# Attention and a token/channel mixer on one core: a hand-set issue order on four engines, strided heads in even steps, the tail product on doubled columns, byte-wise weight conversion

## The chip, the cores and the metric

The kernel runs on one core of one Trainium2 chip, as one program. The metric is device time in microseconds from start to end of the program, the median of several runs. The engines are named as the profile names them: PE multiplies matrices (PEld loads its weights), DVE, ACT and POOL work element-wise, SP issues all DMAs of this kernel. Each engine executes its own list of instructions in a fixed order, and semaphores hold an instruction until what it reads is there.

## The reference

```python
# q, k, v: batch 8, heads 8, sequence 576, head size 64, float32
scores = q @ k.T / sqrt(64)
rel = pos[:, None] - pos[None, :]
mask_local   = (rel >= 0) & (rel < 32)                         # heads 0 to 3
mask_strided = (rel >= 0) & (pos[None] % 32 == pos[:, None] % 32)   # heads 4 to 7
attn = softmax(where(mask, scores, -1e9));  x = heads_side_by_side(attn @ v)   # (8, 576, 512)

xt = x.transpose(0, 2, 1)
h  = relu(xt @ w_tok1) @ w_tok2             # 576 -> 256 -> 576, along the sequence
u  = x + h.transpose(0, 2, 1)
out = u + relu(u @ w_ch1) @ w_ch2           # 512 -> 1536 -> 512, along the channels
```

## The kernel before

**Products in three terms.** Every big product is computed as high*high + high*low + low*high of float32 values split in two, so each weight matrix lies in SBUF as a high and a low tile (w1h and w1l, w2h and w2l, t1, t2). The weights come as raw 64-bit values. `convert` makes float32 words of a piece of 128x512: on ACT one Abs with a scale (L87), on DVE three bit operations (L88, L89, L90). `load_split` then rounds to the high tile on ACT (L101) and subtracts on POOL for the low one (L102). There are 24 such pieces for w1 and w2, and six smaller ones for the token weights.

**Passes.** The channel mixer `mlp` runs nine passes. Passes 0 to 7 take positions 0 to 511 of one batch each, and pass 8 takes the last 64 positions (the tail) of all eight batches. A pass has 24 blocks of 12 matmuls with 512 columns: 12 blocks `up_proj` (L450) and 12 blocks `down_proj` (L462), in the order up 0, up 1, up 2, down 0, up 3, down 1 and so on. After an up block ACT makes gh (L453) and DVE makes gl (L454), which the down block of the same number reads four blocks later. Two PSUM buffers (ps_h) hold the up products.

**Work between the blocks.** During a pass other work is inserted for later passes:

- `tok1` (28 matmuls of 512 columns for a batch, L322) and `tok2` (L345, L337) make the u of the next batch. Before each tok1 step ACT and DVE split a slice of x (L310, L313, L317). `tok2` handles 128 channels at a time: four transposes and six matmuls of 512 columns.
- `tok2_tail` makes the tail of u: for each of four channel groups one transpose (L359) and six matmuls with only 64 columns (L337), kept in the tile utail.
- `local_unit` is local attention for 384 positions of two heads: 24 score matmuls on each of two halves (L133), mask and maximum on DVE (L142), exp on ACT (L145), z on DVE (L148, L149), three transposes (L153), a copy (L155), 48 matmuls (L161), a scaling on DVE (L172). Eighteen units of three chunks fall into the passes.
- Strided attention of batches 0 and 1 runs on PE (`strided_pe`), that of batches 2 to 7 on POOL and DVE (`strided`): for each i from 0 to 17 POOL multiplies i+1 rows (L275), DVE sums them (L276); then a softmax; then 18 products and sums again (L290, L291). A k tile shares its buffer with the output tile of the batch before (sb).

Local and strided results go to HBM and come back as the tile x (`load_x`), of which there is one buffer.

**What sets the order.** Up to the first pass and in the passes, a scheduler orders the instructions of each engine from the calls in the source, their priorities and its own model of time. `at(fc, f)` only says after which up block the source calls an insertion. The strided batches are recorded with a priority lowered by 3000. Local units, tok1, tok2 and the tail share two PSUM buffers (ps_t). Pieces of the weights are called two for each of the first nine fc of pass 0, and the PE-strided lanes of batch 1 in the same pass.

## Time and profile before

| what | value |
|---|---|
| median of 3 runs | 926.01 us (925.93 to 929.34) |
| the profiled execution, whole | 926.17 us |
| its span, first to last instruction | 924.4 us |
| PE busy, share of the span | 850.3 us, 92% |
| DVE, ACT, POOL busy | 479.4, 240.3, 398.9 us |
| mean granted clock of PE | 0.943 |

Matmuls overlap in the pipeline, so "busy" of PE says only when it had something in flight. How fast it goes is read from the distance between the starts of matmuls, and where it stands from the idle time before an instruction, which the views give in brackets with the instruction that ended it. A clock of 1.00 is 2.4 GHz, and 0.5 is 1.2 GHz.

### The profile page before, as it was taken

To read this page: it belongs to the slowest core of one execution; us is meant where nothing else is said; L and a number is where in the kernel's file an instruction comes from. 1 tells how busy PE (TensorE), PEld (TensorE's weight loads), DVE (VectorE), ACT (ScalarE), POOL (GpSimd) and SP (SyncE) were. 2 spreads that over 40 slices of the span, in tenths; PEclk is the share of its full clock that TensorE was granted. 3 is DMA by queue.
4 is the path that set the end of the run, shared out by engine and by line. 5 is a ranking of instruction groups with operands and counts; after the bars stand their busy time and mean duration, and the time that the engine had idled before them with its cause. 6 is when DMAs were issued, how large, how long until landed. Compare 5 with 4: busy or idle time off the path is not lost.

```text
span 924.4 us, 15050 instructions
## 1 busy us (share of the span) xinstructions
PE 850.3 (92%) x5964; PEld 684.7 (74%) x5964; DVE 479.4 (52%) x1133; ACT 240.3 (26%) x700; POOL 398.9 (43%) x291
## 2 busy tenths in 40 slices
PE   5897899569998599999998899999999999999997
PEld 4675688448776487877786678878887888888885
DVE  3969782277648747765775565766223112213111
ACT  5656452122222222222221221232122111111110
POOL 0324540098746848768795765967002000100000
PEclk9568999769999799999999799999999999999999
DMA  8665641411332351133315313042103000001002
GB/s 249 185 220 158 212 128 45 137 46 44 98 116 87 107 146 50 52 114 100 99 27 162 105 45 103 30 133 80 46 1 111 1 1 23 23 1 44 3 0 46
DMA packets 65635, 78.03 MB, mean 84 GB/s; under 512 B 23076, under 2 KB 50340, under 8 KB 65564
## 3 DMA queue, kind: packets, MB, share of 16 engines
q1 hardware_dynamic: 65564, 77.07, 27.7%
q8 instruction: 47, 0.77, 0.4%
q14 instruction: 24, 0.20, 0.1%
HBM read 58.63 MB, written 18.28 MB: 83 GB/s over the span
## 4 chain that ended last, share of the span: by engine, by line
PE 61%; POOL 13%; DVE 10%; DMA 8%; SPq 3%; issue 2%; ACT 2%; POOLq 0%; ACTq 0%; DVEq 0%
PE h L450 25%; PE acc L462 24%; POOL sprod L275 7%; POOL sprod L290 6%; PE t L337 5%; DMA sb<-in_ks 3%; PE t L322 2%; DMA x<-xs 2%; PE t L345 2%; DVE xlo L313 1%; DVE ss L276 1%; DVE w_f L89 1%; DVE w_f L88 1%; DVE lz L148 1%; DMA w_raw<-in_wt 1%
## 5 line engine op out<-in xcount | busy, mean ns | idle before, releaser
L275 POOL TENSOR_TENSOR sprod<-sb,sa 128x64 f32<-128x64 f32 (+8 forms) x108 | 159.5, 1513 | 103.4 <-DMA sb<-in_ks 52.7
L454 DVE SCALAR_TENSOR_TENSOR gl<-h,gh 128x512 fp32r<-128x512 f32 x108 | 74.1, 688 | 208.8 <-ACT gh L453 208.4
L290 POOL TENSOR_TENSOR sprod<-sa,ss 128x64 f32<-128x64 f32 (+8 forms) x108 | 155.0, 1476 | 38.8 <-DVE ss L285 33.5
L462 PE MATMUL acc<-gl,w2h 128*128 128x512 f32 x432 | 171.0, 396 | 0.0
L450 PE MATMUL h<-ul,w1h 128*128 128x512 f32 x432 | 170.4, 395 | 0.5 <-DVE ul L350 0.4
L450 PE MATMUL h<-uh,w1h 128*128 128x512 f32 x432 | 167.1, 396 | 3.8 <-DVE gl L454 3.8
L450 PE MATMUL h<-uh,w1l 128*128 128x512 f32 x432 | 170.1, 394 | 0.0
L462 PE MATMUL acc<-gh,w2l 128*128 128x512 f32 x432 | 169.9, 393 | 0.0
L462 PE MATMUL acc<-gh,w2h 128*128 128x512 f32 x432 | 166.5, 399 | 3.3 <-ACT gh L453 3.3
L453 ACT ACTIVATE gh<-h 128x512 fp32r<-128x512 f32 x108 | 63.8, 596 | 344.9 <-PE h L450 344.9
L473 POOL TENSOR_TENSOR ot<-uh,ul 128x512 f32<-128x512 f32 x32 | 42.8, 1343 | 158.1 <-DMA out_t<-ot 79.8
L276 DVE TENSOR_REDUCE ss<-sprod 128x1 f32<-128x64 f32 (+8 forms) x108 | 84.3, 782 | 49.1 <-POOL sprod L275 48.5
L291 DVE TENSOR_REDUCE sb<-sprod 128x64 f32<-128x64 f32 (+8 forms) x108 | 84.2, 782 | 34.5 <-POOL sprod L290 33.3
L450 PEld LDWEIGHTS h<-uh,w1h 128*128 128x128 f32 x432 | 81.6, 190 | 22.2 <-DVE gl L454 4.7
L462 PEld LDWEIGHTS acc<-gh,w2h 128*128 128x128 f32 x432 | 81.0, 189 | 21.8 <-ACT gh L453 4.3
L450 PEld LDWEIGHTS h<-ul,w1h 128*128 128x128 f32 x432 | 81.9, 190 | 18.6 <-DVE ul L350 1.4
L450 PEld LDWEIGHTS h<-uh,w1l 128*128 128x128 f32 x432 | 81.9, 190 | 17.4
L462 PEld LDWEIGHTS acc<-gl,w2h 128*128 128x128 f32 x432 | 81.1, 188 | 17.4
L462 PEld LDWEIGHTS acc<-gh,w2l 128*128 128x128 f32 x432 | 81.1, 188 | 16.8
L145 ACT ACTIVATE ls<-ls,lm 128x64 f32<-128x64 f32 x144 | 48.3, 337 | 44.6 <-DVE lm L142 44.3
L322 PE MATMUL t<-xh,t1h 128*128 128x512 f32 (+1 forms) x90 | 34.3, 413 | 18.1 <-ACT xh L310 12.8
L337 PE MATMUL t<-t2h,hh 128*128 128x64 f32 (+1 forms) x128 | 49.1, 383 | 0.0
(86 smaller groups left out, 1013.8 us busy)
## 6 DMA issues: line engine op xcount, KB each, us to landing
w_raw<-in_w SPq DMA_DIRECT2D x24, 512.0 KB
out_t<-ot SPq DMA_DIRECT2D x32, 256.0 KB
lv<-in_vw SPq DMA_DIRECT2D x20, 384.0 KB
lk<-in_kT SPq DMA_DIRECT2D x20, 208.0 KB
x<-xs SPq DMA_DIRECT2D x8, 512.0 KB
lq<-in_qT SPq DMA_DIRECT2D x20, 192.0 KB
x<-xl SPq DMA_DIRECT2D x7, 512.0 KB
sa<-in_qs SPq DMA_DIRECT2D x6, 576.0 KB
```

What stands on the lines that cost most here:

```text
L145: nc.scalar.activation(out=s_t[:, c, j, :], in_=s_t[:, c, j, :], func=AF.Exp, bias=m_t[:, c, j:j + 1], scale=-1.0, accum_out=z_t[:, c, j:j ...
L275: nc.gpsimd.tensor_tensor(out=pr, in0=k_t[:, :n, :], in1=q_t[:, i:i + 1, :].to_broadcast([P, n, D]), op=ALU.mult)
L276: nc.vector.tensor_reduce(out=s_t[:, i, :n], in_=pr, axis=AX.X, op=ALU.add)
L290: nc.gpsimd.tensor_tensor(out=pr, in0=v_t[:, :, :n], in1=s_t[:, i:i + 1, :n].to_broadcast([P, D, n]), op=ALU.mult)
L291: nc.vector.tensor_reduce(out=o_t[:, i], in_=pr, axis=AX.X, op=ALU.add)
L322: nc.tensor.matmul(ph[m], l[:, c, ms], r, start=(c == 0 and k == 0), stop=(c == NSC - 1 and k == 1))
L337: nc.tensor.matmul(pu, l[:, cs], r[:, m, ts], start=False, stop=(m == 1 and k == 2), skip_group_check=True)
L450: nc.tensor.matmul(ph, l[:, cc, fs], r, start=(cc == 0 and k == 0), stop=(cc == NCC - 1 and k == 2))
L453: nc.scalar.activation(out=gh, in_=ph, func=AF.Relu)
L454: nc.vector.scalar_tensor_tensor(out=gl, in0=ph, scalar=0.0, in1=gh.bitcast(F32), op0=ALU.max, op1=ALU.subtract)
L462: nc.tensor.matmul(acc[cc], l[:, fc, cs], r, start=(fc == 0 and k == 0), stop=(fc == NFC - 1 and k == 2))
L473: nc.gpsimd.tensor_tensor(out=o_t, in0=uh.bitcast(F32), in1=ul.bitcast(F32), op=ALU.add)
```

## The change

**Order.** From the passes on (the prologue keeps the scheduler) PE, DVE, ACT and POOL issue in the order of the source. SP is still ordered by the scheduler. `mlp` calls `done` after each block, and insertions stand in tables of block numbers 0 to 23: the local units in `UNITS`, tok1 at blocks 14 to 19 (15 to 19 in passes 0 and 1), tok2 at 20 to 23, the tail product after block 0 of the batch's own pass, weight pieces one for each of the blocks 0 to 15 of pass 0, the PE-strided lanes of batch 1 in its blocks 1 to 12.

**Strided heads.** `strided` becomes a generator whose steps multiply two rows that together have 18 (8; 7 and 9; 6 and 10; ...; 17), and whose sums stand one step behind. `some_strided` calls 22/20 of a step's worth for each block in passes 0 and 1, and 22/23 later. q, k, v and the output share three buffers.

**Tail.** `tok2_tail` puts h on the weight side: six matmuls of 512 columns against a t2 with the 64 tail columns doubled, a DVE addition onto x, and a DMA of 64 rows to HBM. In pass 7 all tails are loaded and transposed by 16 transposes (`tail_u`).

**Weights.** `convert` builds the low bits and the sign with byte accesses: a new Identity on ACT (L96), a byte-wise and on DVE (L97), then Abs (L99) and a single combining DVE operation (L100), in place of three.

**Smaller moves.** z and its reciprocal stand after the transposes' copy; tok1 splits two slices ahead; local units have two buffers for k and v.

```diff
-        nc.vector.tensor_scalar(out=a, in0=a, scalar1=3, scalar2=None, op0=ALU.logical_shift_left)
-        nc.vector.scalar_tensor_tensor(out=a, in0=low, scalar=29, in1=a, op0=ALU.logical_shift_right, op1=ALU.bitwise_xor)
-        nc.vector.scalar_tensor_tensor(out=a, in0=high, scalar=0x80000000, in1=a, op0=ALU.bitwise_and, op1=ALU.bitwise_xor)
+        nc.scalar.activation(out=y_b[:, :, 0], in_=raw_b[:, :n, 3], func=AF.Identity, bias=below, scale=1.0 / 32)
+        nc.vector.tensor_scalar(out=y_b[:, :, 3], in0=raw_b[:, :n, 7], scalar1=128, scalar2=None, op0=ALU.bitwise_and)
...
+        nc.vector.scalar_tensor_tensor(out=a, in0=a, scalar=3, in1=y, op0=ALU.logical_shift_left, op1=ALU.bitwise_xor)
...
+    STEPS = ((8,),) + tuple((i, NJ - 2 - i) for i in range(7, -1, -1)) + ((NJ - 1,),)
...
+            late = []
+            for step in STEPS:
+                pr, at = pool.tile([P, NJ * D], F32, name="sprod", bufs=2), 0
+                now = []
+                for i in step:
+                    now.append((i, pr[:, at:at + (i + 1) * D]))
+                    product(*now[-1])
+                    at += (i + 1) * D
+                for l in late:
+                    add(*l)
+                late = now
+                yield at / (NJ * D)
...
+        for m in range(2):
+            hh, hl = h[m]
+            for k, (l, r) in enumerate(((t2h, hh), (t2l, hh), (t2h, hl))):
+                nc.tensor.matmul(pu, l[:, m, MAIN:], r, start=(m == 0 and k == 0), stop=(m == 1 and k == 2))
+        rs = slice(64 * (b % 2), 64 * (b % 2) + 64)
+        nc.vector.tensor_tensor(out=x_t[rs, NSC - 1], in0=pu[rs], in1=x_t[rs, NSC - 1], op=ALU.add)
+        nc.sync.dma_start(out=ud[b], in_=x_t[rs, NSC - 1])
...
+        for p in range(B // 2):
+            nc.tensor.transpose(pu[:, P * p:P * p + P], u_t[:, p, P * cc:P * cc + P], ident)
+        return split_u(pool, pu)
...
+    ordered = {mybir.EngineType.PE, mybir.EngineType.DVE, mybir.EngineType.Activation, mybir.EngineType.Pool}
+    ctx.enter_context(tc.manual_schedule(engines=ordered))
...
+    def some_strided(blocks):
+        turn["owed"] += 22.0 / blocks
...
+    UNITS = {1: ((0, 1, 3, 4), (0, 3, 5, 6), (2, 5, 8, 9), (4, 8, 10, 11)),
+             2: ((0, 2, 5, 6), (0, 4, 8, 9), (4, 7, 11, 12), (6, 10, 12, 13)),
...
+        at(0, tok2_tail, ps_t, x_t, h, b)
+        if b + 1 < B:
+
+            local, stride, steps = (12, 13, (15, 16, 17, 18, 19, 19)) if b < 2 else (11, 11, range(14, 20))
+            at(min(local, stride), load_next, b + 1)
+            at(local, load_half, b + 1, 0)
+            at(stride, load_half, b + 1, 1)
+            for i in steps:
+                at(i, do_tok1)
+            for cc in range(NCC):
+                at(20 + cc, do_tok2, cc)
...
+        if b == 0:
+            for i in range(16):
+                at(i, do_pieces, 1)
```

**ACT in pass 0, where the weight pieces are converted.** L87 or L99 is Abs, L96 the new Identity, L101 or L111 the rounding to the high tile, L453 or L535 makes gh, and L227, L239 are the exps of the PE-strided heads. Before:

```order
L453 ACTIVATE gh<-h 128x512
L87 ACTIVATE w_f<-w_raw 128x512 x2
L227 ACTIVATE es,em<-es,em 126x126 x4
L227 ACTIVATE es,em<-es,em 72x72
L101 CAST w1h<-w_f 128x512
L453 ACTIVATE gh<-h 128x512
L101 CAST w2h<-w_f 128x512
L87 ACTIVATE w_f<-w_raw 128x512 x2
```

After:

```order
L535 ACTIVATE gh<-h 128x512
L96 ACTIVATE w_rest_103<-w_raw,below 128x512
L99 ACTIVATE w_f<-w_raw 128x512
L111 CAST w1h<-w_f 128x512
L239 ACTIVATE es,em<-es,em 126x126 x4
L239 ACTIVATE es,em<-es,em 72x72
L535 ACTIVATE gh<-h 128x512
L96 ACTIVATE w_rest_102<-w_raw,below 128x512
L99 ACTIVATE w_f<-w_raw 128x512
L111 CAST w2h<-w_f 128x512
```

Before, other instructions of ACT stand between Abs and the cast of the same piece; now the cast follows its Abs directly.

**PE at the end of pass 3** (acc is the down product, lv the values of a local unit, x and hh belong to tok2 of the next batch). Before:

```order
L462 MATMUL acc_3422<-gh,w2l 128x512
L161 MATMUL t<-lv,ls 32x64 x24
L345 MATMUL t<-ident,x 128x128 x4
L337 MATMUL t<-t2h,hh_3874 128x512
L337 MATMUL t<-t2l,hh_3874 128x512
```

After, at the end of pass 1 (from pass 1 on every pass ends in this way up to pass 6), with the tail product further on:

```order
L545 MATMUL acc_2143<-gh,w2l 128x512
L404 MATMUL t<-ident,x 128x128 x4
L408 MATMUL t<-t2h,hh_2770 128x512
L408 MATMUL t<-t2l,hh_2770 128x512
L408 MATMUL t<-t2h,hl_2771 128x512
L408 MATMUL t<-t2h,hh_2772 128x512
L408 MATMUL t<-t2l,hh_2772 128x512
L408 MATMUL t<-t2h,hl_2773 128x512
L532 MATMUL h<-uh,w1h 128x512
```

The local unit's last matmuls have moved away from the end of the pass to its blocks 4 to 13.

**POOL, strided products of the first batch that POOL computes** (sprod is the product; ot the sum uh + ul that the output needs). Before:

```order
L275 TENSOR_TENSOR sprod<-sb,sa 128x1088
L473 TENSOR_TENSOR ot<-uh,ul 128x512
L275 TENSOR_TENSOR sprod<-sb,sa 128x1152
L473 TENSOR_TENSOR ot<-uh,ul 128x512 x3
L290 TENSOR_TENSOR sprod<-sa,ss 128x64
L290 TENSOR_TENSOR sprod<-sa,ss 128x128
```

After, the second of these batches:

```order
L312 TENSOR_TENSOR sprod<-sa 128x576
L312 TENSOR_TENSOR sprod<-sa 128x512
L312 TENSOR_TENSOR sprod<-sa 128x640
L549 TENSOR_TENSOR ot<-uh,ul 128x512
L312 TENSOR_TENSOR sprod<-sa 128x448
L312 TENSOR_TENSOR sprod<-sa 128x704
```

Long and short products now alternate, and the sums ot stand singly between them.

## Rows read from the trace of the kernel before

**Rows 1.** The page: the span, and busy time of PE with its share and instructions.

```profile
span 924.4 us, 15050 instructions
PE 850.3 (92%) x5964; PEld 684.7 (74%) x5964; DVE 479.4 (52%) x1133; ACT 240.3 (26%) x700; POOL 398.9 (43%) x291
```

**Rows 2.** Windows by pass: stretch, its us, busy by engine (instructions), PEclk, DMA share, GB/s.

```profile
87.00:171.00 84.00, 80.35 (x407) 65.53 (x402) 50.78 (x134) 34.31 (x93) 27.82 (x20) 0.98 0.40 125
171.00:209.00 38.00, 19.66 (x153) 14.54 (x152) 19.86 (x44) 7.24 (x21) 23.16 (x17) 0.64 0.31 101
209.00:322.00 113.00, 99.56 (x881) 77.73 (x880) 76.76 (x172) 27.74 (x91) 79.21 (x58) 0.92 0.32 92
512.00:609.00 97.00, 92.60 (x683) 74.07 (x682) 63.75 (x128) 22.36 (x65) 66.28 (x46) 0.96 0.29 85
609.00:699.00 90.00, 89.57 (x683) 72.40 (x683) 37.74 (x94) 21.53 (x63) 30.86 (x23) 1.00 0.21 60
```

**Rows 3.** PE's waits: line <- releaser, us in total, times, longest.

```profile
PE t L345 <- DVE lx L172: 11.1, 6, 3.8
```

**Rows 4.** The chain that ended last: start, us, what.

```profile
852.61 5.44 PE h L450 x24
874.37 2.72 PE h L450 x12
```

**Rows 5.** Timeline of PE: start, us, instruction, count, idle time before it and its releaser.

```profile
86.96 0.73 PE L450 MATMUL h<-uh,w1h 128*128 128x512 f32 x2
182.12 1.22 PE L322 MATMUL t<-xh,t1h 128*128 128x512 f32 x2 [10.77 <-ACT xh L310]
209.37 0.27 PE L359 MATMUL t<-ident,x 128*128 128x128 f32 x1
212.33 0.48 PE L450 MATMUL h<-ul,w1h 128*128 128x512 f32 x1
505.61 1.12 PE L345 MATMUL t<-ident,x 128*128 128x128 f32 x4 [3.80 <-DVE lx L172]
628.81 0.49 PE L153 MATMUL t<-ident,ls 128*128 128x128 f32 x3
653.43 0.72 PE L161 MATMUL t<-lv,ls 64*32 64x64 f32 x48
773.89 0.60 PE L345 MATMUL t<-ident,x 128*128 128x128 f32 x4
775.72 0.60 PE L345 MATMUL t<-ident,x 128*128 128x128 f32 x4
```

**Rows 6.** Groups of ACT by shape: count, busy us, mean ns of one, idle time before.

```profile
L87 ACT ACTIVATE w_f<-w_raw 128x512 f32<-128x512 f32 x28 | 18.7, 673 | 16.8 <-DMA w_raw<-in_wt 5.7 <-DMA w_raw<-in_w 5.5 <-POOL w2l L102 2.8
L101 ACT CAST w2h<-w_f 128x512 fp32r<-128x512 f32 x12 | 7.4, 618 | 13.7 <-DVE w_f L90 13.7
L227 ACT ACTIVATE es<-es,em 126x126 f32<-126x126 f32 x32 | 12.5, 392 | 8.5 <-DVE em L224 8.5
L227 ACT ACTIVATION_READ_ACCUMULATOR es<-es,em 126x1 f32 x32 | 6.0, 188 | 0.0
L453 ACT ACTIVATE gh<-h 128x512 fp32r<-128x512 f32 x108 | 63.8, 596 | 344.9 <-PE h L450 344.9
```

**Rows 7.** Groups of DVE by shape, in the same columns.

```profile
L90 DVE SCALAR_TENSOR_TENSOR w_f<-w_raw,w_f 128x512 uint32<-128x512 uint32 x28 | 22.8, 815 | 0.2
L88 DVE TENSOR_SCALAR w_f<-w_f 128x512 uint32<-128x512 uint32 x28 | 15.8, 564 | 9.9 <-ACT w_f L87 9.7
```

**Rows 8.** Groups of POOL: the products over all shapes (page), and ot.

```profile
L275 POOL TENSOR_TENSOR sprod<-sb,sa 128x64 f32<-128x64 f32 (+8 forms) x108 | 159.5, 1513 | 103.4 <-DMA sb<-in_ks 52.7
L290 POOL TENSOR_TENSOR sprod<-sa,ss 128x64 f32<-128x64 f32 (+8 forms) x108 | 155.0, 1476 | 38.8 <-DVE ss L285 33.5
L473 POOL TENSOR_TENSOR ot<-uh,ul 128x512 f32<-128x512 f32 x32 | 42.8, 1343 | 158.1 <-DMA out_t<-ot 79.8 <-DVE ul L350 76.1 <-DVE sz L283 2.2
```

**Rows 9.** Timeline of DVE: a six-column operation while POOL multiplies.

```profile
281.76 2.92 DVE L148 TENSOR_SCALAR lz<-lz 128x6 f32<-128x6 f32 x1 [0.36 <-ACT ls L145]
```

More of the change, by code (lines that the diff above doesn't have):

```diff
@@ L163, in local_unit @@
                     pT[64 * j:64 * j + 64, 32 * t:32 * t + 32], v_t[64 * j:64 * j + 64, t], start=True, stop=True)
-        x_t = pool.tile([P, max(n - 1, 2) if into is not None or n < UC else UC, 2, D], F32, name="lx")
+        x_t = pool.tile([P, max(n - 1, 2) if into is not None or n < UC else UC, 2, D], F32, name="lx", bufs=one.get("lx"))
         cs = slice(P * hp, P * hp + P)
@@ L305, in tok1, with split @@
         n = cs.stop - cs.start
-        ph = [ps_t.tile([P, 512], F32, name="t")[:, :n] for _ in range(2)]
-        for c in range(NSC):
+        def split(c):
             x = x_t[:, c, cs]
@@ L331, in new_h, with split_u, tok2 @@
         return [[pool.tile([P, DM], F32R, name=f"h{k}{m}", bufs=1) for k in "hl"] for m in range(2)]
-    def tok2_terms(h, pu, cs, ts):
+    def split_u(pool, pu):
+        uh = pool.tile([P, MAIN], F32R, name="uh", bufs=NCC)
+        ul = pool.tile([P, MAIN], F32R, name="ul", bufs=NCC)
+        nc.scalar.copy(out=uh, in_=pu)
+        nc.vector.tensor_tensor(out=ul, in0=pu, in1=uh.bitcast(F32), op=ALU.subtract)
+        return uh, ul
+    def tok2(pool, ps_t, x_t, h, cc):
+        cs = slice(P * cc, P * cc + P)
+        pu = ps_t.tile([P, 512], F32, name="t")
+        for c in range(NSC - 1):
+            nc.tensor.matmul(pu[:, P * c:P * c + P], x_t[:, c, cs], ident, is_transpose=True, start=(c == 0), stop=False, skip_group_check=True)
         for m in range(2):
@@ L487, in out_tail @@
         nc.sync.dma_start(out=to[:, :, MAIN:], in_=o_t.rearrange("p (b t) -> p b t", t=TAIL))
-    def do_load(b):
-        state["x"] = xp.tile([P, NSC, DM], F32, name="x", bufs=1)
-        for half in range(2):
-            load_x(state["x"], b, half)
-        state["h"] = new_h(xp)
-        state["tok1"] = tok1(xp, ps_t, state["x"], state["h"], slice(0, DM))
-        state["next"] = []
-    def do_tok1():
-        next(state["tok1"], None)
-    def do_tok2(*ccs):
-        state["next"] += tok2(up0, ps_t, state["x"], state["h"], ccs)
@@ L503, in do_tail @@
-    def do_tail(b):
-        tok2_tail(ps_t, state["x"], state["h"], b, range(NCC))
-    def tail_group():
-        us = []
-        for cc in range(NCC):
-            uh = up0.tile([P, MAIN], F32R, name="uh", bufs=NCC)
-            ul = up0.tile([P, MAIN], F32R, name="ul", bufs=NCC)
-            nc.scalar.copy(out=uh, in_=u_tail[:, cc])
-            nc.vector.tensor_tensor(out=ul, in0=u_tail[:, cc], in1=uh.bitcast(F32), op=ALU.subtract)
-            us.append((uh, ul))
-        return us
-    def step(g):
-        return lambda: next(g, None)
@@ L536, in attn_mixer_kernel, with strided_lane @@
-    pools = {}
-    def second_ends():
+    def strided_lane(pool, b, gs, got):
+        for hp in range(HL // 2):
+            if hp not in got:
+                got[hp] = strided_load(pool, b, hp), {}
+            for j in range(2):
+                yield from strided_pe(pool, ps_t, b, hp, j, gs, *got[hp])
+    pools = {}
+    pools["second"] = tc.tile_pool(name="second", bufs=2, reuse_waits="tile")
+    second, got = pools["second"].__enter__(), {}
+    lanes = [strided_lane(second, 1, gs, got) for gs in GS]
@@ L539, in second_ends, with first_ends, staging_ends @@
+    def first_ends():
+        for g in lanes:
+            assert next(g, lanes) is lanes
         pools.pop("second").__exit__(None, None, None)
+    def staging_ends():
+        assert not pieces and "second" not in pools
+        staging.__exit__(None, None, None)
         pools["sp"] = ctx.enter_context(tc.tile_pool(name="sp", bufs=1, reuse_waits="tile"))
-        do_strided(NSB)
-    def staging_ends():
-        assert not pieces
-        staging.__exit__(None, None, None)
-        pools["late"] = ctx.enter_context(tc.tile_pool(name="late", bufs=1, side="right", reuse_waits="tile"))
@@ L606, in attn_mixer_kernel @@
-    mlp(state["u"], {}, out_tail, [u_tail[:, cc] for cc in range(NCC)])
+        pools["late"] = ctx.enter_context(tc.tile_pool(name="late", bufs=2, side="right", reuse_waits="tile"))
+    turn = dict(batch=NSB, gen=None, owed=0.0)
+    def some_strided(blocks):
+        turn["owed"] += 22.0 / blocks
+        while turn["owed"] > 0 and turn["batch"] < B:
+            if turn["gen"] is None:
+                turn["gen"] = strided(pools["sp"], turn["batch"])
+            n = next(turn["gen"], None)
+            if n is None:
+                turn["batch"] += 1
+                turn["gen"] = None
+            else:
+                turn["owed"] -= n
@@ L609 @@
+    mlp(u, {}, out_tail)
 _OUT = (DM, B * S)
```

265 lines of the change are left out of this document (133 added, 132 removed), and 4 rows, old and new, of the table UNITS.

## The prediction, made before the changed kernel was run

> **What bounds the kernel now.** I read the page first, then PE's time by pass, then the idle time inside it. PE is busy for 850.3 of 924.4 us [rows 1], and the chain that ended last is mostly up and down blocks, but busy time does not say how fast PE goes. The undisturbed rate is seen at the end of the chain: 12 matmuls of 512 columns start within 2.72 us [rows 4], 0.227 us each at a clock of 1.00. At that rate a pass of 24 blocks takes 24 x 2.72 = 65.3 us, and nine of them 588 us.
>
> The windows by pass show what is lost [rows 2]. From 171 to 209 us PE is busy for 19.7 of 38 us at a mean clock of 0.64: it stands 10.77 us for the x of batch 1 [rows 5], and after that hole works partly at 1.2 GHz. The stretch 209 to 322 holds one pass and its insertions and takes 113 us at 0.92; 512 to 609 takes 97 us at 0.96; 609 to 699, with the same 683 matmul records, takes 90 us at 1.00. So an equal load costs 7 us more where PE had holes. One cause repeats: six times tok2 waits for the scaling of a local unit (11.1 us together [rows 3]), because the unit's last product stands just ahead of tok2 in PE's list and holds both buffers of ps_t. At 505.61 this is a hole of 3.80 us [rows 5]. PE is the bound, and the orders of the other engines decide its holes.
>
> **The change part by part.** First the PE work that stays. tok1 is 28 matmuls, 28 x 0.227 = 6.35 us for each batch. A channel group of tok2 takes 775.72 - 773.89 = 1.83 us [rows 5], so four take 7.3 us. A local unit is 48 score matmuls, three transposes and 48 matmuls. The last two are busy for 0.49 and 0.72 us [rows 5]; with the scores taken like the last product it is 1.93 us, less overlap 1.9.
>
> *Tail product.* The old one stands from 209.37 to 212.33, 2.96 us on PE [rows 5]. The new one is 6 x 0.227 = 1.36 us, plus 16 transposes once. From tok2's step, (1.83 - 1.36) / 4 = 0.12 us each, so 1.9 us. Eight batches: 23.7 - 10.9 - 1.9 = 10.9 us less PE work. Its DVE addition and DMA are followed by nothing urgent: x is next written ten blocks later.
>
> *Order in the passes.* Units end by block 13, tok1 has ps_t alone in blocks 14 to 19, tok2 has it in 20 to 23. This takes away the hole before tok2. The x loads are called at block 11 (12 and 13 in passes 0 and 1), and the split of x that needs them at 14 or 15, three or two blocks later, 8 or 5 us and more. What becomes late next is ACT or DVE behind a neighbour in its list. A gl is needed four blocks after its up block, and PSUM is needed back after three: 3 x 2.72 = 8.2 us of cover. From the stretch 609 to 699 I take what remains in a pass without holes: 90.0 - (65.3 + 6.35 + 7.3 + 2.96 + 3 x 1.9) = 2.4 us; I use 2.0, since the units no longer meet tok2.
>
> *Strided heads.* POOL's products are 159.5 + 155.0 us for six batches, 52.4 us each, and ot adds 4 x 1.34 = 5.4 us a pass [rows 8]. POOL also stood 52.7 us for k and 33.5 us for the softmax in all, 14.4 us a batch. That makes 72 us of POOL for each batch as the waits are now. A batch gets 20 blocks of a pass in the first passes and 23 later, and by the sums below these take PE 20/24 of 92 us, 76 us, or 23/24 of 88, 84 us. The k tile no longer waits until the last output is written; if that takes a third off its 8.8 us a batch, POOL needs 69 us. So POOL keeps up, by some 10% where it is tightest. What hides it is DVE's cover of 8.2 us; if that cover is gone, DVE stands in order behind a sum, gl comes late, and PE waits.
>
> *Weights.* DVE loses two operations of 0.815 us and one of 0.564 [rows 7], and gains a byte-wise one and one combining. ACT gains an Identity. The byte-wise prices are not in the trace. The nearest rows are L88 at 0.564 us on DVE and Abs at 0.673 us on ACT [rows 6, 7], for equal element counts. Bounds: half of that, since the bytes are a quarter, and twice that. A gain beyond that is excluded, as each still touches 512 elements. I take the nearest rows, so a piece costs DVE 1.38 in place of 2.19 us. But on ACT the cast of a piece now follows its Abs directly, and ACT must wait for DVE's combining operation. A piece holds ACT for 0.673 + 0.673 + 0.815 + 0.618 = 2.78 us [rows 6, 7]. In blocks 0 to 15 of pass 0 that is 16 x 2.78 = 44.5 us. There are also nine gh of 0.596 (5.4 us) and four rounds of PE-strided lanes: five exps of 0.392 + 0.188, 2.9 us, and copies that I estimate at 0.95 us from the same row, 15.4 us together. ACT needs 65.3 us, where PE needs 16 x 2.72 + 1.36 and about 6.2 for the lanes, 51 us. **In these 16 blocks ACT is the new bound.** With Identity at half or twice its price it would be 60 or 76 us.
>
> *Pass 0 and before it.* The first up block stands at 86.96 us [rows 5]. Fewer DVE operations in the prologue may move it by some us: I take 85, bounds 79 to 91. Then 65.3, the split of the first slice 1.6, and blocks 16 to 23: 21.8 + 6.35 + 7.3 = 35.4. A PE that ACT holds in small pieces may get the lower clock for a part, as in 171 to 209; I allow 5 us. Pass 0 ends at 85 + 65.3 + 1.6 + 35.4 + 5 = 192.3, where the old one reaches 209.
>
> *The sum.* Passes 1 and 2 have four units: 65.3 + 6.35 + 7.3 + 1.36 + 7.6 = 87.9, with 2.0 left over 89.9. Pass 1 gets 2 us more, because the strided batch 2 ends only at block 11 and its x must be written and read before block 15. Passes 3 to 5 have three units: 88.0 each. Pass 6 has one: 84.2. Pass 7 has none, but the tails: 65.3 + 1.4 + 1.9 + 0.4 = 69.0. Together 91.9 + 89.9 + 264.0 + 84.2 + 69.0 = 599.0. The last pass is untouched, and from its start at 852.61 to the end of the span it takes 71.8 us [rows 1, 4]. Outside the span lie 926.2 - 924.4 = 1.8 us. 192.3 + 599.0 + 71.8 + 1.8 = 864.9, and the median stands 0.2 below the profiled execution. I predict **864.5 us**, a ratio of 0.934.
>
> **A row that speaks against it.** At 281.76 a DVE operation on six columns takes 2.92 us [rows 9], about the length of one POOL product: DVE seems held until POOL is through. The Trainium skill (SBUF — State Buffer, "Who interferes with whom") says that DVE and GpSimd share a port pair by an exclusive lock, which DVE wants when it has two SBUF inputs or a 2-port mode, and that the other one blocks for the whole instruction; it excludes tensor_reduce. By that rule the even steps, which keep POOL multiplying in most blocks, expose every split of x and every z to such a hold, and the time would be that of the first rival below. The row agrees with it for z.
>
> **The rivals.**
>
> *Holes at the hand-over.* In each of passes 1 to 5 DVE stands behind POOL twice in a row (a sum that waits for a late k, then a z or split held 2.9 us), the cover of 8.2 us is used up, and PE has one hole of about 4 us. After such a hole the clock was lower in the old trace, and 97 against 90 us is what holes cost in a pass [rows 2]. So 5 x 8 = 40 us more: 905 us. For it speaks POOL's thin margin; against it that z now stands behind the transposes' copy, off the path to PE. Chance 0.20.
>
> *A better pass 0.* ACT's waits for DVE fall into time when it would wait for PE anyhow, and nothing falls to the lower clock: 864.5 - 14 = 850 us. Chance 0.10.
>
> *The order does little.* The holes move to other places and only the tail's 10.9 us are won: 915 us. Against it speaks that the old holes have a nameable cause that the tables remove. Chance 0.05.
>
> *Slower than before.* POOL paces PE. The sums stand in DVE's list between gl and gl, so if a step of two products takes POOL longer than PE's block and its share of insertions, PE goes at POOL's rate for six batches. The margin is 76 - 69 = 7 us a batch. To end at the old time, each batch would have to take 7 + 61.5 / 6 = 17 us longer, from where it decides: products a third slower than the means of 1.5 us [rows 8]. I take it at 940 us. The products' means already hold DVE's present interference, which speaks against it. Chance 0.05.
>
> **How the numbers follow.** The forecast has 0.60. A difference under 0.5%, 4.6 us, is about what a measurement of this kernel can tell from no change. The range takes in the better pass 0 and its bounds below and the hand-over case above: 846 to 908 us, which leaves out the last two cases and a little of the others' edges. Faster by over 0.5%: the forecast, both neighbours and nearly all of the little-order case, 0.93. Within 0.5%: 0.03. Slower: 0.04, most of the POOL case.
>
> **What would show it.** Right: PE without holes over 2 us in passes 2 to 6, windows of 84 to 91 us a pass at a clock near 1.00; pass 0 from first up block to pass 1 in 100 to 112 us, with ACT over 80% busy or waiting for the combining operation in its first two thirds; the tail product at 1.4 us; Identity near 0.67 us and the byte-wise and near 0.56. Wrong: PE waiting for gl or gh in every pass while DVE waits for POOL's sprod (hand-over or POOL case); the wait for x of batch 1 still near 10 us; an up block that starts after 95 us; Identity above 1.3 us.

## The result

The changed kernel takes **869.49 us** (median of four runs, 867.93 to 870.86); the kernel before took 925.97 us in the same comparison. The ratio is 0.938, with a 95% interval of 0.9355 to 0.9408. The forecast was 864.5 us, with a range from 846 to 908. The profiled execution took 869.74 us, its span 867.9. Two executions far above the others of their kernel (3943.2 us of before_shift32, 869.5 of best) stand outside the medians and ranges given below.

The page of the changed kernel, to be read beside [rows 1]:

```profile
span 867.9 us, 14809 instructions
PE 833.8 (96%) x5804; PEld 659.8 (76%) x5804; DVE 452.3 (52%) x1111; ACT 257.5 (30%) x722; POOL 408.8 (47%) x298
PE 84%; ACT 6%; DMA 4%; DVE 2%; SPq 1%; issue 1%; DVEq 0%
```

The last line is the chain that ended last. Before the change it read:

```profile
PE 61%; POOL 13%; DVE 10%; DMA 8%; SPq 3%; issue 2%; ACT 2%; POOLq 0%; ACTq 0%; DVEq 0%
```

Now it is PE for 84% of the span, and POOL has gone from it. PE's own idle time, summed over the trace, falls from 67.5 to 27.9 us.

Windows by pass, in the columns of [rows 2]: pass 0 in three stretches, then passes 1 to 7, each from its first up block to the next one's. The first stretch is the end of the prologue, in which six of the 12 matmuls of up block 0 already stand; from 83.0 us on the blocks follow each other.

```profile
70.00:84.00 14.00, 13.13 (x191) 9.59 (x175) 6.19 (x33) 6.49 (x25) 0.00 (x0) 1.00 0.16 43
84.00:144.00 60.00, 58.75 (x289) 45.29 (x289) 33.88 (x117) 43.14 (x105) 21.64 (x16) 1.00 0.57 170
144.00:182.00 38.00, 36.87 (x167) 29.31 (x166) 22.52 (x33) 9.97 (x17) 29.53 (x22) 1.00 0.29 105
182.00:280.00 98.00, 93.24 (x759) 73.02 (x758) 66.19 (x146) 24.43 (x77) 64.96 (x46) 0.98 0.33 96
280.00:372.40 92.40, 90.90 (x761) 71.43 (x760) 58.35 (x139) 23.98 (x76) 64.60 (x46) 1.00 0.33 98
372.40:461.90 89.50, 88.83 (x661) 70.18 (x660) 60.21 (x124) 21.61 (x63) 64.26 (x46) 1.00 0.30 89
461.90:550.40 88.50, 88.50 (x661) 70.21 (x660) 57.45 (x122) 21.62 (x63) 61.16 (x44) 1.00 0.31 90
550.40:639.60 89.20, 88.70 (x660) 70.38 (x659) 57.72 (x123) 21.51 (x63) 63.56 (x46) 1.00 0.27 76
639.60:724.10 84.50, 84.50 (x463) 67.69 (x462) 24.96 (x51) 16.08 (x36) 8.53 (x6) 1.00 0.16 44
724.10:794.30 70.20, 70.20 (x311) 56.57 (x310) 13.22 (x20) 9.41 (x16) 5.04 (x4) 1.00 0.08 26
```

Three things are to be seen. The clock is 1.00 in pass 0 and from pass 2 on; only pass 1 has a dip. In passes 4, 6 and 7 PE is busy for the whole window. And pass 0 ends at 182.0, ten us earlier than forecast, while the passes behind it take 15 us more than forecast. The kernel before ended pass 0 at 209 us [rows 2], so 27 of the 56 us are won by then.

The group of [rows 3], PE waiting for a unit's scaling before tok2, is gone. The two largest of PE's waits over the whole span are now these:

```profile
PE t L145 <- DMA lk<-in_kT: 6.1, 2, 4.0
PE t L380 <- ACT xh L362: 5.1, 3, 3.6
```

The first lies before 84 us. Of the second, the single 3.6 us is the one large hole left behind the prologue. On PE's timeline in pass 1 it stands before tok1 of batch 2, and the matmuls behind it (0.43 us from one start to the next in place of 0.23) run at 1.2 GHz; the granted clock is at that level for 3.4 us:

```profile
244.81 0.80 PE L380 MATMUL t<-xh,t1h 128*128 128x512 f32 x1 [3.57 <-ACT xh L362]
246.13 0.63 PE L380 MATMUL t<-xh,t1l 128*128 128x512 f32 x1
246.56 0.63 PE L380 MATMUL t<-xh,t1h 128*128 128x512 f32 x1
```

The end of the chain, to be read beside [rows 4], shows what nobody had foreseen: 12 matmuls of 512 columns take 2.80 us at a clock of 1.00, where 12 took 2.72 before:

```profile
847.76 2.80 PE acc L545 x12
850.56 2.80 PE h L532 x12
```

That is 0.2333 us a matmul in place of 0.2267. In the last pass nothing is inserted and PE never waits, so no neighbour explains it. The difference that suggested itself was where the tiles lie in SBUF. A matmul reads two of them: its weights, and the moving operand, which is streamed past the weights. The new constant tile `below`, for which 32 bytes a partition are set aside, moves all tiles allocated behind it (x, h, xh, xlo, uh, ul, gh, gl) by 32 bytes against the weights. Before the change the distance in SBUF from the weight tiles to these moving operands was a multiple of 1024 bytes. (Places are those of the allocation; a trace does not show them.)

### The profile page after: what moved, and what is told of

Read it like the earlier page. It is cut to its first block, busy times and chain, and to the rows that moved or that the text cites. A ratio compares the mean times of both kernels' runs of the same rounds, so it can differ in the third digit from the quotient of the medians.

```text
span 867.9 us, 14809 instructions
## 1 busy us (share of the span) xinstructions
PE 833.8 (96%) x5804; PEld 659.8 (76%) x5804; DVE 452.3 (52%) x1111; ACT 257.5 (30%) x722; POOL 408.8 (47%) x298
## 4 chain that ended last, share of the span: by engine, by line
PE 84%; ACT 6%; DMA 4%; DVE 2%; SPq 1%; issue 1%; DVEq 0%
PE h L532 33%; PE acc L545 32%; PE t L380 6%; PE t L408 5%; PE t L404 2%; PE t L145 2%; PE t L173 2%; ACT w_rest L96 1%; PE t L417 1%; DMA x<-xs 1%; DMA w_raw<-in_wt 1%; ACT es L239 1%; ACT w_f L99 1%; ACT ls L157 1%; DVE w_f L100 1%
## 5 line engine op out<-in xcount | busy, mean ns | idle before, releaser
L335 POOL TENSOR_TENSOR sprod<-sa,ss 128x576 f32<-128x576 f32 (+8 forms) x108 | 154.6, 1458 | 94.6 <-issue 49.5
L312 POOL TENSOR_TENSOR sprod<-sa 128x576 f32<-128x576 f32 (+8 forms) x108 | 162.7, 1534 | 50.5 <-DVE ss L317 30.3
L545 PE MATMUL acc<-gh,w2h 128*128 128x512 f32 x432 | 174.4, 404 | 0.0
L532 PE MATMUL h<-uh,w1h 128*128 128x512 f32 x432 | 173.5, 402 | 0.0
L535 ACT ACTIVATE gh<-h 128x512 fp32r<-128x512 f32 x108 | 64.5, 598 | 331.4 <-PE h L532 331.4
L549 POOL TENSOR_TENSOR ot<-uh,ul 128x512 f32<-128x512 f32 x36 | 49.5, 1387 | 140.5 <-DMA out_t<-ot 140.5
L340 DVE TENSOR_REDUCE sa<-sprod 128x64 f32<-128x576 f32 (+8 forms) x108 | 79.4, 776 | 3.0 <-POOL sprod L335 2.9
L317 DVE TENSOR_REDUCE ss<-sprod 128x9 f32<-128x576 f32 (+8 forms) x108 | 79.4, 775 | 2.2 <-POOL sprod L312 2.0
L397 DVE TENSOR_TENSOR ul<-t,uh 128x512 fp32r<-128x512 f32 x36 | 24.9, 691 | 56.4 <-ACT uh L396 56.4
L396 ACT CAST uh<-t 128x512 fp32r<-128x512 f32 x36 | 21.1, 587 | 103.6 <-PE t L408 95.7
```

The costliest lines, as they stand in the source:

```text
L312: nc.gpsimd.tensor_tensor(out=pr.rearrange("p (n d) -> p n d", d=D), in0=k_t[:, :n, :], in1=q_t[:, i:i + 1, :].to_broadcast([P, n, D]), op ...
L317: nc.vector.tensor_reduce(out=s_t[:, i, :i + 1], in_=pr.rearrange("p (n d) -> p n d", d=D), axis=AX.X, op=ALU.add)
L335: nc.gpsimd.tensor_tensor(out=pr.rearrange("p (d n) -> p d n", n=n), in0=v_t[:, :, :n], in1=s_t[:, i:i + 1, :n].to_broadcast([P, D, n]), o ...
L340: nc.vector.tensor_reduce(out=o_t[:, i], in_=pr.rearrange("p (d n) -> p d n", n=i + 1), axis=AX.X, op=ALU.add)
L532: nc.tensor.matmul(ph, l[:, cc, fs], r, start=(cc == 0 and k == 0), stop=(cc == NCC - 1 and k == 2))
L535: nc.scalar.activation(out=gh, in_=ph, func=AF.Relu)
```

## The experiments

Times are medians; the changed kernel stands at 869.5. Each ratio is to the kernel before, measured on the same chip. The chips differ by up to 1.8 us in the kernel before, so that a difference between two medians below can be off by as much.

### Where the tiles lie

**align64.** The constant tile takes 64 bytes.

```diff
-    below = const.tile([P, 1], F32, name="below")
+    below = const.tile([P, 16], F32, name="below")[:, :1]
```

> The changed kernel with one edit: the constant tile below is 64 bytes wide in place of 32, so that every tile allocated after it (x, h, xh, xlo, uh, ul, gh, gl) starts at a multiple of 64 bytes again, as in the kernel before; nothing else moves. In the changed kernel they start at 32 mod 64, and its 512-column matmuls start every 0.2333 us at a clock of 1.00, against 0.2267 before. Theory (start address of the moving operand): the step is 0.2267 us again; about 3056 such matmuls x 0.0066 us = 20 us less, 848 to 852 us; a pass without insertions from 67.4 back to 65.5 us. Rival (the chip of that run, or something else in the change, makes PE slower): step 0.2333 and 868 to 871 us, unchanged.

Measured: 861.1 us (860.4 to 863.2), ratio 0.929 [0.927, 0.931]. Neither number came: the gain is 8 us of the 20 that the theory wanted, and the block of 12 lies between the two.

```profile
837.91 2.75 PE h L532 x12
840.66 2.75 PE acc L545 x12
```

So the place of the tiles matters, but "a multiple of 64" is not the rule.

**before_shift32.** The kernel before, with 32 unused bytes ahead of pool xp.

```diff
+    pad = const.tile([P, 8], F32, name="pad")
+    nc.gpsimd.memset(pad, 0.0)
     xp = ctx.enter_context(tc.tile_pool(name="xp", bufs=2))
```

> The kernel before with one edit: an unused constant tile of 32 bytes ahead of pool xp, which shifts x, h, xh, xlo, uh, ul, gh and gl to 32 mod 64 bytes. Theory (start address): the step of the 512-column matmuls goes from 0.2267 to 0.2333 us at a clock of 1.00, about 3008 x 0.0066 = 20 us, of which some falls into holes: 940 to 946 us. Rival (chip, or something else in the change): step 0.2267 and 924 to 929 us.

Measured: 939.6 us (935.6 to 941.1), ratio 1.0125 [1.010, 1.015], and a block of 2.80 us where the kernel before has 2.72 [rows 4]:

```profile
913.41 2.80 PE acc L464 x12
916.21 2.80 PE h L452 x12
```

Neither the chip nor anything else in the change is needed: 32 unused bytes in the old program make its matmuls as slow as those of the changed one. It costs 12.5 us of the 20 us worked out. PE of that program stands in holes for 65 us; that the rest of the longer step falls into them is likely, but not shown.

**up_off32.** align64, with gh, gl and ot moved by another 32 bytes.

```diff
+    off = up.tile([P, 8], F32, name="off", bufs=1)
+    nc.gpsimd.memset(off, 0.0)
     ps_acc = ctx.enter_context(tc.tile_pool(name="ps_acc", bufs=1, space=PSUM, reuse_waits="tile"))
```

> The kernel of align64, with 32 unused bytes at the start of pool up alone: gh, gl and ot lie at 32 mod 64, while uh, ul, xh, xlo and h lie at 0. Theory (start address of the matmul's moving operand): down blocks (moving operands gh, gl) at 2.80 us, up blocks (uh, ul) at 2.72 us, 1296 x 0.0066 = 8.6 us above align64, 856 to 861 us. Rival (the place of any other tile, for example of the weights' staging or of what ACT and DVE write): up and down blocks alike, either both 2.72 or both 2.80 us.

Measured: 866.7 us (865.8 to 868.9), ratio 0.935 [0.933, 0.937], above the 856 to 861 of the theory. Up and down blocks now differ within one pass:

```profile
841.05 2.76 PE h L534 x12
843.81 2.80 PE acc L547 x12
```

The down blocks, whose moving operands gh and gl were shifted, take 2.80 us; the up blocks, with uh and ul left where they were, 2.76, close to the 2.75 of align64. So it is the moving operand's own place that counts. The theory's 2.72 for the up blocks was wrong, as in align64, and with it the time.

**align128.** The constant tile takes 128 bytes.

```diff
+    below = const.tile([P, 32], F32, name="below")[:, :1]
```

> The changed kernel with the constant tile below widened to 128 bytes, so that x, h, xh, xlo, uh, ul, gh and gl start at multiples of 128 bytes, as in the kernel before. Seen so far in the last undisturbed stretches: matmul step 0.2268 us with starts at 0 mod 128 (before), 0.229 at 64 (align64), 0.2332 at 32 (the change and before_shift32), 0.2335 at 96 (down blocks of up_off32). Theory (start address, in 128 bytes): step 0.2268 us, another 2.2 ns x 3056 = 6.7 us off align64, 851 to 856 us. Rival (the rest of the step comes from something else in the changed program): step 0.229 and 859 to 863 us, as align64.

Measured: 868.4 us (865.1 to 870.7), ratio 0.936 [0.933, 0.938]. A miss: 2.80 us again, though every moving operand starts at a multiple of 128 and of 256 bytes. Absolute alignment to 128 bytes is not the rule.

**below_in_staging.** The constant tile goes to the staging pool at the other end of SBUF, and nothing is left between weights and moving tiles.

```diff
-    below = const.tile([P, 1], F32, name="below")
+    below = stage.tile([P, 1], F32, name="below", bufs=1)
```

> The changed kernel with the 32-byte constant tile below allocated in the staging pool at the other end of SBUF, so that x, h, xh, xlo, uh, ul, gh and gl start at 128 mod 256 bytes, at a distance from the weights that is a multiple of 1024 bytes, both as in the kernel before. Seen so far: matmul step 0.2268 us with starts at 128 mod 256 (before), 0.229 at 192 (align64), 0.2332 at 160 (the change and before_shift32), 0.2335 at 224 (down blocks of up_off32), 0.2331 at 0 (align128); the weights lie at 128 mod 256 in all of them. Theory (the place of the moving operand, absolute in 256 bytes or as a distance from the weights): step 0.2268 us, 3056 x 6.4 ns = 20 us off the change, 847 to 853 us. Rival (something else in the changed program makes the step longer): step 0.229 us or more, 859 to 870 us.

Measured: **855.0 us** (853.5 to 856.1), ratio 0.922 [0.920, 0.924]; the blocks are back at 2.72 us:

```profile
834.52 2.72 PE acc L545 x12
837.24 2.72 PE h L532 x12
```

This is faster than both kernels. The step is the one expected; the time stands 2 us above the theory's range, since passes 0 and 1 together gain only 2 us. In pass 1 the hole before tok1 stays (3.08 us), and in this execution 6.8 us at half clock follow. What PE waits for there is ACT's split of x, and ACT waits for the load of x:

```profile
240.59 0.62 ACT L362 CAST xh<-x 128x512 fp32r<-128x512 f32 x1 [7.21 <-DMA x<-xs]
```

**all_shift32.** below_in_staging with 32 bytes ahead of the weights: weights and moving tiles shift alike.

```diff
+    pad = const.tile([P, 8], F32, name="pad")
+    nc.gpsimd.memset(pad, 0.0)
     w1h = const.tile([P, NCC, DF], F32R, name="w1h")
```

> The kernel of below_in_staging with 32 unused bytes ahead of the weights, so that weights and moving operands shift alike: all at 160 mod 256 bytes, their distance still a multiple of 1024. Theory A (the distance between moving operand and weights decides): step 0.2268 us, 847 to 853 us. Theory B (the absolute place of the moving operand decides): step 0.2332 us, as in the change, 867 to 872 us.

Measured: 856.8 us (856.1 to 858.1), ratio 0.925 [0.922, 0.927], and 2.72 us for 12. Here the moving operands lie at 160 mod 256 bytes, exactly where the changed kernel has them with 2.80. So theory A holds: the distance between the matmul's moving operand and its weights decides, not the absolute place. The tiles at the other end of SBUF stayed where they were, so the distance to them does not decide either. Its time, too, is a little above the range that both theories took over from below_in_staging.

### The parts of the change

**no_hand_order.** The scheduler orders the four engines again.

```diff
-    ctx.enter_context(tc.manual_schedule(engines=ordered))
```

> The changed kernel without the order set by hand: the scheduler orders PE, DVE, ACT and POOL again, and tables, tail product, conversion and even steps stay. Theory (the order, with the tables, is what removes PE's holes): holes come back where a neighbour in the list is late; the hole-free passes 2 to 6 lose 3 to 8 us each and pass 0 some, 895 to 925 us. Rival (the order does little, the tail product and the tables of insertions bring the gain): 866 to 878 us.

Measured: 908.5 us (903.0 to 910.0), ratio 0.979 [0.976, 0.982]: by hand the order is worth 39 us here, the largest part. PE's waits and three windows (passes 0 to 2):

```profile
PE t L380 <- DVE xh L365: 8.8, 4, 3.6
PE t L404 <- DVE hl L388: 5.5, 5, 2.9
PE t L380 <- DVE xlo L368: 4.8, 4, 2.0
72.20:198.00 125.80, 111.50 (x603) 86.92 (x602) 62.50 (x170) 53.70 (x139) 37.68 (x28) 0.90 0.38 117
198.00:300.30 102.30, 95.65 (x759) 73.42 (x758) 74.34 (x153) 24.76 (x77) 75.37 (x54) 0.97 0.32 94
300.30:402.40 102.10, 96.30 (x760) 74.20 (x759) 74.08 (x152) 23.93 (x76) 80.48 (x59) 0.95 0.31 94
```

With the same tables PE waits for the DVE operations that tok1 and tok2 need, the mean clock of a pass falls to 0.90 to 0.97, and passes 0, 1 and 2 are 14, 4 and 10 us longer than in the changed kernel. The rival "the order does little" falls.

**old_tail.** The tail product of before: per batch four transposes and 24 matmuls of 64 columns, gathered through DRAM.

```diff
...
-                nc.tensor.matmul(pu, l[:, m, MAIN:], r, start=(m == 0 and k == 0), stop=(m == 1 and k == 2))
...
+                    nc.tensor.matmul(pu[:, P * cc:P * cc + TAIL], l[:, cs], r[:, m, MAIN:MAIN + TAIL], start=False, stop=(m == 1 and k == 2), skip_group_check=True)
...
```

> The changed kernel with the old tail product: per batch four transposes and 24 matmuls of 64 columns, an ACT copy, a DMA of the four token tails to DRAM; they are loaded again in pass 7, whose 16 transposes fall away. Addresses of all other tiles as in the change. Theory (PE is the bound without holes, so PE work counts in full): 8 x (2.96 - 1.40) - 1.9 = 10.6 us more, 878 to 882 us. Rival (part of it lay beside a wait of PE): 869 to 875 us.

Measured: 880.5 us (879.5 to 884.8), 11.0 us above the changed kernel, where the sum said 10.6. Passes 3 to 6, in which PE has no large hole, are each 1.6 to 1.7 us longer than in the changed kernel, which is the 2.96 - 1.40 of the sum: there PE's work counts in full. The total hides two things that nearly cancel: pass 1 is 3.5 us longer, since its hole before tok1 is 5.36 us in this execution with 6.8 us at half clock behind it, and pass 0 ends no later.

**old_conversion.** The three DVE operations of before in place of Identity, byte-and and the combining operation.

```diff
...
-        nc.scalar.activation(out=y_b[:, :, 0], in_=raw_b[:, :n, 3], func=AF.Identity, bias=below, scale=1.0 / 32)
-        nc.vector.tensor_scalar(out=y_b[:, :, 3], in0=raw_b[:, :n, 7], scalar1=128, scalar2=None, op0=ALU.bitwise_and)
...
-        nc.vector.scalar_tensor_tensor(out=a, in0=a, scalar=3, in1=y, op0=ALU.logical_shift_left, op1=ALU.bitwise_xor)
+        nc.vector.tensor_scalar(out=a, in0=a, scalar1=3, scalar2=None, op0=ALU.logical_shift_left)
+        nc.vector.scalar_tensor_tensor(out=a, in0=low, scalar=29, in1=a, op0=ALU.logical_shift_right, op1=ALU.bitwise_xor)
+        nc.vector.scalar_tensor_tensor(out=a, in0=high, scalar=0x80000000, in1=a, op0=ALU.bitwise_and, op1=ALU.bitwise_xor)
```

> The changed kernel with the three DVE operations of the old weight conversion (shift, low bits, sign) after Abs, in place of Identity, byte-and and one combining operation; addresses as in the change. Theory (in blocks 0 to 15 of pass 0 ACT and DVE stand just below PE, ACT busy or waiting for the combining operation for 90% of 83 to 140 us): ACT waits about 2 us per piece for DVE in place of 0.8 and loses 0.88 of Identity, so ACT is about as late as now; DVE has 1 us more per piece; pass 0 gets 0 to 4 us longer and starts up to 3 us later: 870 to 877 us. Rival (conversion was what bounded pass 0, so it wins much): 880 us and more. Second rival (fewer ACT operations help): below 868 us.

Measured: 875.8 us (875.0 to 879.0), 6.3 us above the changed kernel. The waits of ACT between 64 and 150 us:

```profile
ACT w2h L104 <- DVE w_f L93: 17.4, 8, 3.6
ACT w1h L104 <- DVE w_f L93: 13.2, 6, 2.7
```

and the same two in the changed kernel:

```profile
ACT w2h L111 <- DVE w_f L100: 7.6, 10, 0.8
ACT w1h L111 <- DVE w_f L100: 5.2, 6, 1.4
```

ACT saves 24.6 us of Identity in all, but in this stretch it waits 17.8 us longer for DVE. The byte-wise conversion takes DVE off ACT's path; it does not make ACT's own work less.

These prices are each taken with the other parts in place, and they need not add up: 39, 11.0 and 6.3 us already make the 56.5 us that the whole change won, while the shifted tiles cost 14.5.

**single_steps.** One product a step, in rising order.

```diff
-    STEPS = ((8,),) + tuple((i, NJ - 2 - i) for i in range(7, -1, -1)) + ((NJ - 1,),)
+    STEPS = tuple((i,) for i in range(NJ))
```

> The changed kernel with one product a step, rows 0 to 17 in rising order as before the change, on two product buffers; order by hand, tables and all else as in the change; the same products in all, so each batch ends at about the same block. Theory (the cover of DVE, 8.2 us, hides the sums' waits for POOL in either form): 868 to 873 us. Rival (even steps are what keeps POOL level with PE: with single steps two or three small products fall into one block and the large ones into the last blocks, DVE stands behind them and PE waits): holes of 2 to 4 us in passes 1 to 5, 880 us and more.

Measured: 871.9 us, but spread from 867.4 to 878.6; ratio 0.941 [0.937, 0.945]. The median is as the theory said, and the even steps cannot be told from the single ones by time. The profiled execution was the slowest, and it shows the rival's mechanism at work in pass 3. DVE, POOL and PE in the same 7 us:

```profile
426.24 0.69 DVE L536 SCALAR_TENSOR_TENSOR gl<-h,gh 128x512 fp32r<-128x512 f32 x1 [0.84 <-ACT gh L535]
426.85 5.00 DVE L368 TENSOR_TENSOR xlo<-x,xh 128x512 fp32r<-128x512 f32 x1
425.50 4.57 POOL L312 TENSOR_TENSOR sprod<-sa 128x960 f32<-128x960 f32 x2
430.04 1.25 POOL L549 TENSOR_TENSOR ot<-uh,ul 128x512 f32<-128x512 f32 x1
431.90 0.79 PE L380 MATMUL t<-xlo,t1h 128*128 128x512 f32 x1 [3.29 <-DVE xlo L368]
```

The split of x is 0.69 us long where POOL is idle. Here it stands for 5.00 us, until POOL has run through two products and an addition that follow each other without a gap; PE has a hole of 3.29 us, and 6.8 us at half clock follow. gl, just ahead of it, takes its 0.69 us although POOL multiplies.

### The hole in pass 1

**best.** below_in_staging, with the strided heads of the first two passes paced faster and x loaded a block earlier in pass 1.

```diff
-            local, stride, steps = (12, 13, (15, 16, 17, 18, 19, 19)) if b < 2 else (11, 11, range(14, 20))
+            local, stride, steps = (12, 13 - b, (15, 16, 17, 18, 19, 19)) if b < 2 else (11, 11, range(14, 20))
...
-                at(i, some_strided, 20 if b < 2 else 23)
+                at(i, some_strided, 18 if b < 2 else 23)
```

> The kernel of below_in_staging, with the strided heads of the first two passes paced over 18 blocks in place of 20, and the strided half of batch 2's x loaded after block 12 of pass 1 in place of 13. Theory (the hole of 3.57 us in pass 1 and its 3.4 us at half clock come from batch 2's strided heads ending at block 11): the hole goes, 5 us less than below_in_staging, 842 to 848 us, pass 1 at about 91 us. Rival (POOL, pushed closer, holds DVE longer where x is split, and the hole comes back elsewhere): within 2 us of below_in_staging.

Measured: 862.3 us, spread from 855.8 to 866.3; ratio 0.929 [0.925, 0.933]: slower than the kernel that it was to mend, though two executions are as fast as that one. The profiled execution is one of the slow end (865.1 us). The strided output of batch 2 was stored 2 us earlier (from 226.9 us, against 229.0), but its x was not there earlier: the loads stand in SP's queue behind the stores of the last local unit, and the first split starts at 241.6 us, against 240.6. Then, with more products in a block, DVE's list put sums that wait for POOL ahead of the next split, and the split itself was held for 2.2 us; pass 1 has a hole of 5.25 us within tok1. Shifted in time, the other batches met POOL at other points too; in pass 5:

```profile
597.24 5.17 DVE L368 TENSOR_TENSOR xlo<-x,xh 128x512 fp32r<-128x512 f32 x1
595.18 5.46 POOL L335 TENSOR_TENSOR sprod<-sa,ss 128x448 f32<-128x448 f32 x4
600.61 1.25 POOL L549 TENSOR_TENSOR ot<-uh,ul 128x512 f32<-128x512 f32 x1
602.47 0.80 PE L380 MATMUL t<-xlo,t1h 128*128 128x512 f32 x1 [3.56 <-DVE xlo L368]
```

Both the theory and the number of its rival missed; the rival's reason is what the trace shows of the execution that was profiled.

**tok1_later.** below_in_staging, with tok1 one block later in pass 1 alone.

```diff
-            local, stride, steps = (12, 13, (15, 16, 17, 18, 19, 19)) if b < 2 else (11, 11, range(14, 20))
+            local, stride, steps = (12, 13, (15 + b, 16 + b, 17 + b, 18, 19, 19)) if b < 2 else (11, 11, range(14, 20))
```

> The kernel of below_in_staging with one edit in pass 1 alone: tok1 of batch 2 begins one block later (its six steps at blocks 16, 17, 18, 18, 19, 19 in place of 15, 16, 17, 18, 19, 19); loads, strided heads and all else stay. Theory (the hole before tok1 in pass 1, 3.1 to 3.6 us, is x of batch 2 arriving late, and is worth up to 3.4 us more at half clock): the hole falls under 1 us and pass 1 from 98.0 to 92 to 95 us, 849 to 853 us. Rival (what holds tok1 up is DVE, whose split of x, with two SBUF operands, waits for POOL's product in flight, or the sums ahead of it in its list): a hole of 2 us or more stays in pass 1, 853 to 858 us.

Measured: 851.5 us, from 849.6 to 862.1; ratio 0.922 [0.918, 0.926]. In the profiled execution (850.1 us) PE's holes before tok1 are 0.23 and 0.98 us, nothing runs at half clock there, and pass 1 takes 92.7 us in place of 98.0:

```profile
241.36 0.50 PE L380 MATMUL t<-xh,t1h 128*128 128x512 f32 x1 [0.23 <-ACT xh L362]
242.84 0.50 PE L380 MATMUL t<-xlo,t1h 128*128 128x512 f32 x1 [0.98 <-DVE xlo L368]
```

The first split of x starts at 240.7 us here and at 240.6 in below_in_staging: x comes no earlier, but PE asks for it a block later. So the late x was the cause of that hole. As a time it is not settled: the interval overlaps that of below_in_staging, and two of the six executions were above 857 us without a profile to say why.

## Why the prediction was right, and where it was not

The sum said 864.9 for the profiled execution, and it took 869.7. That the total is off by 5 us only is luck: two errors of 10 and 15 us nearly cancel.

**The bound and the holes: right.** PE is the bound, the holes before tok2 are gone (before tok2's transposes, L404, PE idles for less than 0.1 us everywhere), and passes 2 to 6 have no hole over 1.02 us. The wait for the x of batch 1 in pass 0, 10.77 us before [rows 5], is 0.90. no_hand_order shows that it is the order, and not the tables alone, that does it: 39 us. What the tables of insertions bring by themselves was not isolated.

**Tail product: right.** The forecast was 10.9 us less PE work, with the 16 new transposes already taken off; undoing it costs 11.0, and 1.6 us a pass where PE has no holes.

**Pass 0: forecast to end at 192.3, ended at 182.0.** The steady blocks start at 83.0 (forecast 85); blocks 0 to 15 take 61.1 us to 144.1 (forecast 65.3); the rest takes 37.9 (37.0); and the 5 us for the lower clock did not come, the clock is 1.00 throughout. The step that failed is "in these 16 blocks ACT is the new bound", and with it the allowance for the clock that hung on it. PE and ACT are level there. PE is busy for 58.75 of the 60 us to 144. ACT is busy for 43.1 of them, waits about 11 for the combining operation, and has 5.5 us left in which it waits for PE (the waits of ACT between 64 and 150 us):

```profile
ACT gh L535 <- PE h L532: 5.5, 6, 1.6
```

The chain that ended last goes over PE as well as over ACT and the combining operation in this stretch. Two terms were mis-sized, one on each engine. On PE the sum had 51 us, and it took 61: the 15.5 blocks of 2.80 that lie here are 43.4, the tail's product 1.4, and the rest, some 16 us, goes to the PE-strided lanes and to handing over. The lanes' own matmuls are 13.2 us of that from start to start, where the prediction had put 6.2 and named no row for it. On ACT the sum had 65.3 us, where ACT is busy or waiting for the combining operation for about 54. Two errors met in it. Identity costs 877 ns, inside the bounds but well above the nearest row that was taken (673). And durations were added up, although ACT's instructions overlap:

```profile
98.05 0.89 ACT L96 ACTIVATE w_rest<-w_raw,below 128x512 uint8<-128x512 uint8 x1
98.80 0.65 ACT L99 ACTIVATE w_f<-w_raw 128x512 f32<-128x512 f32 x1
100.21 0.62 ACT L111 CAST w1h<-w_f 128x512 fp32r<-128x512 f32 x1 [0.76 <-DVE w_f L100]
```

Identity is 0.89 us long, but Abs starts 0.75 us after Identity does. A piece holds ACT for 2.7 to 2.9 us, so the forecast 2.78 was right by luck: Identity was dearer, the combining operation cheaper (711 ns against 815), and the starts overlap. The exps with their accumulator reads follow each other every 0.39 us in place of 0.58, so that their term was half as long again as it should have been.

**The byte-wise prices.** Three groups of the changed kernel, whose nearest rows were Abs and [rows 7]:

```profile
L96 ACT ACTIVATE w_rest<-w_raw,below 128x512 uint8<-128x512 uint8 x28 | 24.6, 877 | 2.8 <-DMA w_raw<-in_wt 2.0 <-DMA w_raw<-in_w 0.8
L97 DVE TENSOR_SCALAR w_rest<-w_raw 128x512 uint8<-128x512 uint8 x28 | 16.1, 574 | 9.5 <-DMA w_raw<-in_w 4.7 <-DMA w_raw<-in_wt 4.7
L100 DVE SCALAR_TENSOR_TENSOR w_f<-w_f,w_rest 128x512 uint32<-128x512 uint32 x28 | 19.9, 711 | 12.4 <-ACT w_f L99 12.3
```

The byte-and costs what the 32-bit shift did, 574 against 564 ns: a quarter of the bytes saved nothing. The shortest of each, 432 and 411 ns, say the same without the holds by POOL that both means contain. On ACT the byte form costs a third more than Abs.

**Passes 1 to 8: 15.1 us more than forecast.** The step that failed is the first of all, "0.227 us each". It was read from the trace of before and applied to a program in which the same instruction takes 0.2333 us. Passes 2 to 8 take 587.8 us, 8.9 more than the 578.9 of the sum. With the old distance restored they take 576.6, so the longer step costs 11.2 us there, and the other terms of these passes were 2.3 us too high together. Pass 1 has the other 6.1 us: its wait for x was foreseen with 2 us and is 3.57, a stretch of 3.4 us at 1.2 GHz follows, and its matmuls have the longer step too.

**The rivals.** The better pass 0, which had a chance of 0.10, is what came in pass 0 itself, with 10 of its 14 us: nothing fell to the lower clock. The longer step hid it in the total. The holes at the hand-over did not decide, but their mechanism is real. In the changed kernel xlo takes 1.30 us on average against 0.69 undisturbed, and up to 3.17. PE nevertheless idles for only 2.7 us from 272 to 640 us; that this is owed to the two splits by which tok1 is ahead is likely, but no run took that lead away. Two edits that shifted POOL against DVE by a few us (single_steps, best) turned the same hold into holes of 3.3 and 3.6 us. What was held in these traces are DVE operations with two SBUF operands (xlo, the subtraction in the last slice of x), the small additions to z, and the byte-and, which takes 1.42 us here where it takes 0.45 to 0.47 beside an idle POOL:

```profile
105.56 1.42 DVE L97 TENSOR_SCALAR w_rest<-w_raw 128x512 uint8<-128x512 uint8 x1
```

gl and ul, with one operand in PSUM, never took more than 0.69 us, and the sums were not held. That agrees with the rule of the Trainium skill that the prediction weighed (SBUF — State Buffer, "Who interferes with whom"), which names two SBUF inputs or a 2-port mode and leaves out tensor_reduce; whether the additions to z and the byte-and run in such a mode, no run here shows. The measurement adds that such a hold can outlast one POOL operation: 5.00 us, over a product and the two operations behind it. POOL did not pace PE: it is busy for 61 to 65 us of passes of 88 to 98 us.

## What to carry to other kernels

A rate read from the old trace holds only as long as the operands stay where they are: look at the last undisturbed stretch of the new trace first, and keep small constants out of the space between weights and moving tiles. Where a step is moved under an ordered engine, ask for its operands: a two-operand SBUF operation on DVE came as late here as POOL's run of back-to-back work ended, up to 5.2 us, and its cover must be counted in that. Add up ACT's instructions by their starts, not by their durations.
